# Spectral mix and token MLP on one core: the special matrix rows as a compact input of 4 transfers, the sign table as 2, and a layout that counts with 400 GB/s

## The chip, the cores and the metric

One core of a Trainium2 chip runs the whole kernel. The metric is the device time of one execution in microseconds; before the change the median of three runs is 1345.98 us (1345.09 to 1347.06).

## The reference

With x = A_x (1 x 2048 x 1024), four DFT matrices given as inputs, and a second tensor B_x for the MLP's place (the last lines pass x to both halves):

```python
def _A_ref(x, dft_seq_re, dft_seq_im, dft_hid_re, dft_hid_im):
    a = jnp.einsum("bsd,ed->bse", x, dft_hid_re)
    b = jnp.einsum("bsd,ed->bse", x, dft_hid_im)
    y = jnp.einsum("ts,bse->bte", dft_seq_re, a) - jnp.einsum("ts,bse->bte", dft_seq_im, b)
    return y

def _B_ref(x, w1, b1, w2, b2):
    h = _layernorm(x, axis=-1)
    u = jnp.einsum("bsd,sf->bdf", h, w1) + b1
    u = _gelu(u)
    y = jnp.einsum("bdf,fs->bds", u, w2) + b2
    return y.transpose(0, 2, 1)

g = _sigmoid((x * gate_w).sum(-1, keepdims=True))
return g * _A_ref(x, ...) + (1 - g) * _B_ref(x, w1, b1, w2, b2)
```

S is 2048, D 1024, F 3584, all in 32-bit floats.

## The kernel before, in words

The kernel runs four stages one after the other, with their edges overlapping: FastSeq (the DFT along the sequence), FastHid (the DFT along the hidden axis), Up and Down (the two products of the MLP, each a fast bilinear scheme of 26 products). FastSeq and FastHid make use of symmetries of the DFT matrices: a matrix is cut into blocks that are mirror images of one another up to sign, and only one of each set is multiplied. Because the matrices are inputs, the kernel also tests on the chip that the blocks agree (the groups named ne_all and ne_odd on DVE) and falls back to a second, general program if they don't. In normal use that second program doesn't run.

The symmetry fails for a few rows and columns, the special ones: in each block of 256 rows, the first 16 (SPECIAL) stand in for them. FastHid.rows (line 1866) brings these rows in: for each of two halves p a tile fes of 128 x 1024 (8 groups of 16 rows as they are in the matrix) and a tile fer_m of 128 x 512 (what the symmetry says they should be). The difference between them, with a sign from the table rowsign, gives the correction matrix fer (lines 1891 to 1920), which FastHid multiplies at the end. Before, these tiles are filled by small transfers of 16 rows each straight from the matrix ct: 8 of 64 KB into each fes (line 1880) and 16 of 16 KB into each fer_m (line 1887), 48 in all. The sign table rowsign is 128 x 4, one column for each combination of p and t2. DVE fills it with 1 (line 1845), and 24 transfers of one column and 1, 15 or 16 rows each write a -1 or a 0 from a second small table (line 1861). All these small tables lie in one tile, called tiny in the profile.

The tiles that the engines wait for early on are: fx, rows of x (512 KB a transfer, line 609); fc, blocks of the sequence matrix ct (512 KB, also line 609); fc_m, the part of fc that is multiplied, split by ACT (line 636) and DVE (line 643) into a high and a low half; fx_lo, the low half of the combined rows of x, by DVE; fd, blocks of the hidden matrix; qh, the result of FastSeq, stored in HBM; and fq, its way back.

What sets the order: every step of the kernel is a task with engines, an estimated cost, bytes, and a key that says where in the program it belongs. Graph.schedule (line 417) simulates the engines and a single transfer pipe and emits each engine's instructions in the order in which that simulation started them. TensorE's order is fixed by the order of the tasks; the others follow due times (Graph.dues, line 387; a task with a negative key is due before everything else). The pipe moves DMA_RATE bytes per us (line 32), so that constant shifts when a load counts as landed, and with it which ready task an engine takes next. Buffers are slots in two pools; a task that needs a new tile waits in the simulation until a slot is free. Each engine then runs its list strictly in order on the chip. SP issues nearly all loads and the stores of the first two stages, one after the other; a transfer waits on SP for the tiles that it reads or overwrites, and for the transfer issued eight places earlier, whose semaphore it takes over. POOL issues other stores and the transfers that add.

Of the kernel before, what the change touches and what calls it, by code (L numbers as in the profile page):

```python
# [15 lines left out]
P = 128  # L16
S = 2048
D = 1024
F = 3584
H = 512  # L20
# [8 lines left out]


HOP = 0.35
DMA_RATE = 360000.0
SPARE = 2
DMA_LATENCY = 3.5
ADD_LATENCY = 1.5
# [182 lines left out]
SEEN = 1  # L218
LATE = 1
SPECIAL = 16  # L220
LAG = 15
STATS_AT, STATS_STEP = ("y", 1), 4.5
GATE_AT, GATE_STEP = 7, 1.5
GATED_AT, GATED_STEP = 0, 2
# [119 lines left out]
class Graph:  # L344
# [72 lines left out]
    def schedule(self):  # L417
# [44 lines left out]
        def start(t, e):  # L462
# [10 lines left out]
            if t.nbytes:  # L473
                dma = max(dma, now) + t.nbytes / DMA_RATE
                end = dma + DMA_LATENCY + (ADD_LATENCY if t.engines[e] == 0.9 else 0)
# [59 lines left out]
def arm(  # L535
# [2 lines left out]
    x: bass.AP,  # L538
    ct: bass.AP,
    xs: bass.AP,  # L540
    dt: bass.AP,
    w1: bass.AP,
    w2: bass.AP,
# [8 lines left out]
    nc = tc.nc  # L552
    g = Graph(SLOTS)
# [11 lines left out]
    def const(n, name, parts=1):  # L565
        if fast and n < 8:
            if not tiny:
                tiny.extend([consts.tile([P, 32], F32, tag="tiny", name="tiny"), 0])
            tiny[1] += n
            assert tiny[1] <= 32  # L570
            return Buf(None, name, tiny[0][:, tiny[1] - n:tiny[1]], parts)
        return Buf(None, name, consts.tile([P, n], F32, tag=name, name=name), parts)
# [16 lines left out]
    def scratch(n, name, parts):  # L589
        return Buf(None, name, dram.tile([P, n], F32, tag=name, name=name), parts)  # L590
# [15 lines left out]
    def load(key, v, src, r=(), queue="SP"):  # L606
        q = {"SP": nc.sync, "ACT": nc.scalar}[queue]
        dst = (lambda: v.ap.rearrange("p (c j) -> p c j", j=H)) if len(src.shape) == 3 else lambda: v.ap
        g.add({queue: 0.06}, key, lambda e: q.dma_start(dst(), src), r=r, w=(v.reg,), nbytes=P * v.n * 4)
# [37 lines left out]
    step = 0  # L647
# [954 lines left out]
    def cast(key, o, v):  # L1602
        g.add({"ACT": act(v.n)}, key, lambda e: nc.scalar.activation(o.ap, v.ap, AF.Copy), r=(v.reg,), w=(o.reg,))

    def mirror(p, c, q):


        if (p, c, q) == (0, 0, 0):
            return 1, None
        return (1 - 2 * p) * (1 - 2 * c), c if q == 0 else 0  # L1610

    class FastSeq:


# [25 lines left out]
        def matrix(self, p, c, q, kk):  # L1640
# [6 lines left out]
            (s, rep), (turn, half) = mirror(p, c, q), mirror(q, c, p)  # L1647
            first, odd = q == kk == 0, 2 * P - SPECIAL * (p == 0)

# [59 lines left out]
        def special(self, key, c, q, kk, v, s, rep, turn, half, first):  # L1709
# [4 lines left out]
            for t in range(2) if rep is None else (rep,):  # L1714
                model = Buf("h", f"fem{c}{q}{kk}{t}", None, 4)
                for i in range(4):
                    at = i % 2 if rep is None else half
                    src = View(v[0][t], at * 2 * P, SPECIAL)
                    o = View(model, i * SPECIAL, SPECIAL, i)
                    sign = 1 if rep is None else (1 - 2 * q) ** (i // 2) * turn ** (i % 2 != half)  # L1720
# [116 lines left out]
    class FastHid:  # L1837

        def signs_of_rows(self):


            s = const(4, "rowsign")
            low = const(2, "low")
            g.add({"DVE": 0.2}, -1, lambda e: (nc.vector.memset(low.t[:, 0:1], -1.0), nc.vector.memset(low.t[:, 1:2], 0.0)), w=(low,))
            g.add({"DVE": 0.1}, -1, lambda e: nc.vector.memset(s.t, 1.0), w=(s,))
            spans = []
            for p in range(2):
                for c in range(2):
                    (sr, rep), (turn, half) = mirror(p, c, 0), mirror(0, c, p)
                    for b in range(2):  # L1850
                        for t in range(2) if rep is not None else ():
                            at = ((c * 2 + b) * 2 + t) * SPECIAL
                            for t2 in range(2):
                                if t != rep:
                                    spans.append((at, at + 1, 1, p * 2 + t2))
                                if (1 - 2 * p) ** b * sr ** (t != rep) * turn ** (t2 != half) < 0:
                                    spans.append((at + (t != rep), at + SPECIAL, 0, p * 2 + t2))

            def go(_):
                for a, b, k, col in spans:  # L1860
                    nc.sync.dma_start(s.t[a:b, col:col + 1], low.t[a:b, k:k + 1])

            g.add({"SP": 0.06 * len(spans)}, -0.9, go, r=(low,), w=(s,), nbytes=512)
            return s

        def rows(self):

            sign = self.signs_of_rows()
            edge = Buf("f", "fer", None, 2, BF16)
            for p in range(2):  # L1870
                v, model = Buf("f", f"fes{p}", None, 8), Buf("h", f"fer{p}_m", None, 8)
                for c in range(2):
                    (sr, rep), (turn, half) = mirror(p, c, 0), mirror(0, c, p)
                    for b in range(2):
                        for t in range(2):
                            k = (c * 2 + b) * 2 + t
                            at, src = k * SPECIAL, ct[p, c, 0, 0, :SPECIAL]

                            def go(_, at=at, src=src, b=b, t=t, v=v):
                                nc.sync.dma_start(v.t[at:at + SPECIAL, :], src[:, b * 2 + t])  # L1880

                            g.add({"SP": 0.06}, step, go, w=((v, k),), nbytes=SPECIAL * D * 4)
                            for t2 in range(2):
                                tr, tc_ = (t, t2) if rep is None else (rep, half)

                                def go(_, at=at, src=src, t2=t2, tr=tr, tc_=tc_, model=model):
                                    nc.sync.dma_start(model.t[at:at + SPECIAL, t2 * 2 * P:(t2 + 1) * 2 * P],
                                                      src[:, tr, tc_ * 2 * P:(tc_ + 1) * 2 * P])

                                g.add({"SP": 0.06}, step, go, w=((model, k),), nbytes=SPECIAL * 2 * P * 4)  # L1890
                d = Buf("f", f"fed{p}", None, 4)
                for b in range(2):
                    for t2 in range(2):
                        o = View(d, (b * 2 + t2) * 2 * P, 2 * P, b * 2 + t2)
                        a, m = View(v, (b * 2 + t2) * 2 * P, 2 * P), View(model, t2 * 2 * P, 2 * P)
                        col = sign.t[:, p * 2 + t2:p * 2 + t2 + 1]
                        g.add({"DVE": dve(2 * P) + 0.06}, step, lambda e, o=o, a=a, m=m, col=col: nc.vector.scalar_tensor_tensor(
                            o.ap, m.ap, col, a.ap, op0=ALU.mult, op1=ALU.subtract), r=(a.reg, m.reg, sign), w=(o.reg,))
                both = Buf("f", f"feb{p}", None, 2)
                zero, one = View(both, 0, H, 0), View(both, H, H, 1)  # L1900
                g.add({"DVE": dve(H)}, step, lambda e, d=d, zero=zero: nc.vector.scalar_tensor_tensor(
                    zero.ap, d.t[:, :H], -1.0, d.t[:, H:2 * H], op0=ALU.mult, op1=ALU.subtract), r=(d,), w=(zero.reg,))
                sub(step, one, View(v, 0, H), View(v, H, H))
                pieces = []
                for z, part in ((zero, 0), (one, 1)):
                    l, r = View(z.buf, z.c0, 2 * P, part), View(z.buf, z.c0 + 2 * P, 2 * P, part)
                    pieces.append((l, r))
                o = [View(edge, p * D + i * 2 * P, 2 * P, p) for i in range(4)]
                if p == 0:
                    outs = [(pieces[0][0], None, 0), (pieces[0][1], None, 0), (*pieces[1], -1), (*pieces[1], 1)]  # L1910
                else:
                    outs = [(*pieces[al], (1 - 2 * al) * (1 - 2 * c)) for c in range(2) for al in range(2)]
                for i, (l, r, z) in enumerate(outs):
                    if r is None:
                        cast(step, o[i], l)
                        continue
                    m = View(Buf("h", f"feo{p}{i}"), 0, 2 * P)
                    mix(step, m, r, z, l)
                    g.add({"ACT": act(2 * P)}, step, lambda e, o=o[i], m=m: nc.scalar.activation(o.ap, m.ap, AF.Copy, scale=0.5),
                          r=(m.reg,), w=(o[i].reg,))  # L1920
                if p == 0:
                    g.add({"DVE": 0.2}, step, lambda e: nc.vector.memset(
                        edge.t[:, :D].rearrange("p (v i) -> p v i", i=2 * P)[:, :, :SPECIAL], 0.0), r=((edge, 0),), w=((edge, 0),))
            square(step + 1, "rest", View(edge, 0, 2 * D))
            return edge
# [236 lines left out]
        def last(self, p, ih, pairs, got):  # L2162
            for l, r, *to in pairs:
                l, r = (View(got[i], 0, D) for i in (l, r))
                for (b, t2), op in zip(to, (add, sub)):
# [6 lines left out]
                    dst = out_dram[b * 8 + p * 4 + t2 * 2 + ih]  # L2172
                    store(step + LAG + 1, dst.t, dst, View(y, 0, D), "SP")

# [133 lines left out]
```

## Time and profile before

| | us |
|---|---|
| median of 3 runs | 1345.98 |
| lowest, highest | 1345.09, 1347.06 |
| the profiled execution | 1349.58 |
| its span, first to last instruction | 1347.7 |
| PE busy | 1254.7 (93%) |
| DVE busy | 1209.8 (90%) |
| ACT busy | 757.2 (56%) |
| POOL busy | 201.0 (15%) |

The profiled execution moved 369.98 MB, 275 GB/s on average. PE is the matrix engine (TensorE), PEld its weight loads, DVE the vector engine, ACT the scalar engine. SP has no busy time of its own: it only issues transfers, and its rows (SPq) tell when it issued them and for how long it was held. The rows of a wait say which engine and line waited, for whom, how long in total, how often, and the longest. The profile has no chain of waits for this kernel, so the stages are read from the busy times of windows and the waits inside them.

### The profile page before, as it was taken

What the parts mean: (1) busy time and instruction counts of PE and PEld (TensorE: products, weight loads), DVE (VectorE), ACT (ScalarE), POOL (GpSimd) and SP (SyncE); (2) the same over time, 40 slices, a digit from 0 to 9 for tenths busy, and PEclk for the clock granted to TensorE, in tenths of its full rate; (3) what the DMA queues carried; (4) which work ended last, traced back from release to release, by engine and by line L of the source; (5) the groups of instructions that cost most, each with busy time, mean ns of one, the idle gap of its engine ahead of it and who ended that gap; (6) DMA issues with size and microseconds to landing.
All of it is one profiled execution on the core that took longest, in us unless ns stands there. A gap on an engine that the chain in (4) does not pass through costs nothing.

```text
span 1347.7 us, 18830 instructions
## 1 busy us (share of the span) xinstructions
PE 1254.7 (93%) x6082; PEld 1015.1 (75%) x6093; DVE 1209.8 (90%) x1993; ACT 757.2 (56%) x1344; POOL 201.0 (15%) x313
## 2 busy tenths in 40 slices
PE   7398656799999999999999999999999999999997
PEld 5298641466877888888888888888878888888986
DVE  7679769859999997999999995989999989999996
ACT  5558437975556454335356374684864646666543
POOL 0000000000111121212122032321321010232112
PEclk8699777899999999999999999999999999999999
DMA  9598889528687776998899599999998385989564
GB/s 378 178 337 348 290 287 390 161 91 316 229 321 262 259 287 207 350 350 322 316 357 393 181 362 402 369 288 346 297 333 285 102 252 140 278 202 304 134 183 97
DMA packets 153865, 369.98 MB, mean 275 GB/s; under 512 B 19484, under 2 KB 22428, under 8 KB 153756
## 3 DMA queue, kind: packets, MB, share of 16 engines
q1 hardware_dynamic: 123068, 284.44, 59.8%
q0 software_dynamic: 30544, 84.17, 21.9%
q8 instruction: 50, 0.82, 0.2%
q14 instruction: 59, 0.48, 0.1%
q10 hardware_dynamic: 144, 0.07, 0.0%
HBM read 278.68 MB, written 89.92 MB: 274 GB/s over the span
## 4 chain that ended last, share of the span: by engine, by line


## 5 line engine op out<-in xcount | busy, mean ns | idle before, releaser
L1039 PE MATMUL ps_u_p<-u_p_r_hi,u_p_w_hi 128*128 128x512 f32 x728 | 284.9, 391 | 2.5 <-DVE u_c L1092 2.5
L1040 PE MATMUL ps_u_p<-u_p_r_lo,u_p_w_hi 128*128 128x512 f32 x728 | 284.4, 391 | 1.7 <-DVE u_p_r_lo L643 1.7
L1041 PE MATMUL ps_u_p<-u_p_r_hi,u_p_w_lo 128*128 128x512 f32 x728 | 284.2, 390 | 0.0
L1039 PE MATMUL ps_o_p<-o_p_r,o_p_w 128*128 128x512 f32 x654 | 255.2, 390 | 1.7 <-DVE o_c L1092 1.7
L1041 PE MATMUL ps_o_p<-o_p_r,o_p_w 128*128 128x512 f32 x654 | 254.6, 389 | 0.6 <-DVE o_p_w L641 0.6
L1040 PE MATMUL ps_o_p<-o_p_r,o_p_w 128*128 128x512 f32 x654 | 254.6, 389 | 0.2 <-DVE o_p_r L643 0.2
L636 ACT ACTIVATE u_p_w_hi<-u_W_p 128x896 fp32r<-128x896 f32 x104 | 97.5, 950 | 128.0 <-PE ps_u_p L1040 40.7
L1039 PEld LDWEIGHTS ps_u_p<-u_p_r_hi,u_p_w_hi 128*128 128x128 f32 x728 | 137.2, 188 | 32.8 <-DVE u_c L1092 4.3
L1040 PEld LDWEIGHTS ps_u_p<-u_p_r_lo,u_p_w_hi 128*128 128x128 f32 x728 | 137.3, 189 | 30.7 <-DVE u_p_r_lo L643 2.5
L1041 PEld LDWEIGHTS ps_u_p<-u_p_r_hi,u_p_w_lo 128*128 128x128 f32 x728 | 137.3, 189 | 28.6
L1039 PEld LDWEIGHTS ps_o_p<-o_p_r,o_p_w 128*128 128x128 f32 x654 | 122.8, 188 | 29.5 <-DVE o_c L1092 4.3
L1589 PE MATMUL ps_fq<-fc_m,fx_hi 128*128 128x256 f32 (+1 forms) x512 | 115.2, 322 | 30.7 <-ACT fc_m L636 23.4
L1041 PEld LDWEIGHTS ps_o_p<-o_p_r,o_p_w 128*128 128x128 f32 x654 | 122.7, 188 | 26.6 <-DVE o_p_w L641 1.0
L1040 PEld LDWEIGHTS ps_o_p<-o_p_r,o_p_w 128*128 128x128 f32 x654 | 122.8, 188 | 25.7 <-DVE o_p_r L643 0.7
L636 ACT ACTIVATE o_p_w<-o_W_p 128x512 fp32r<-128x512 f32 x164 | 99.8, 625 | 63.7 <-DVE o_W_p L604 28.4
L636 ACT ACTIVATE o_p_r<-o_R_p 128x512 fp32r<-128x512 f32 x157 | 95.4, 624 | 70.3 <-DVE o_R_p L604 37.3
L1589 PEld LDWEIGHTS ps_fq<-fc_m,fx_hi 128*128 128x128 f32 x512 | 92.0, 213 | 36.5 <-ACT fc_m L636 25.0
L619 POOL DMA_DIRECT2D u<-u_c x126 | 68.0, 540 | 308.5 <-DVE u_c L1092 116.3
L643 DVE TENSOR_TENSOR o_p_r<-o_R_p,o_p_r 128x512 fp32r<-128x512 f32 x157 | 106.8, 686 | 5.2 <-ACT o_p_r L636 5.1
L1092 DVE SCALAR_TENSOR_TENSOR u_c<-ps_u_p,u_c 128x512 f32<-128x512 f32 x161 | 105.6, 685 | 4.8 <-PE ps_u_p L1041 3.5
L1589 PE MATMUL ps_fq<-fc_m,fx_lo 128*128 128x256 f32 (+1 forms) x256 | 83.1, 325 | 16.9 <-DVE fx_lo L643 16.9
L601 DVE TENSOR_TENSOR u_W_p<-u_W_p,u_W_p 128x896 f32<-128x896 f32 x80 | 85.8, 1086 | 2.2 <-DMA u_W_p<-in_w_dram 2.2
(258 smaller groups left out, 2217.9 us busy)
## 6 DMA issues: line engine op xcount, KB each, us to landing
u_W_p<-in_w_dram SPq DMA_DIRECT2D x136, 448.0 KB, 6.7
o_W_p<-in_w_dram SPq DMA_DIRECT2D x160, 256.0 KB, 6.6
o_R_p<-u SPq DMA_DIRECT2D x140, 256.0 KB, 5.6
fc<-in_ct_dram SPq DMA_DIRECT2D x64, 512.0 KB, 9.6
u<-u_c POOLq DMA_DIRECT2D x126, 256.0 KB, 5.8
u_c<-u SPq DMA_DIRECT2D x70, 256.0 KB, 7.3
fx<-in_x_dram SPq DMA_DIRECT2D x32, 512.0 KB, 9.0
o_W_p<-in_w_dram POOLq DMA_DIRECT2D x50, 256.0 KB, 7.4
```

Of the source, the lines that this page charges most:

```text
L601: g.add({"DVE": dve(o.n)}, key, lambda e: nc.vector.tensor_add(o.ap, a.ap, b.ap), r=(a.reg, b.reg), w=(o.reg,))
L619: g.add({queue: 0.6 if queue == "POOL" else 0.06}, key, lambda e: q.dma_start(dst, v.ap), r=(v.reg,), w=(reg,) if reg else (), nbytes=P * ...
L636: g.add({"ACT": act(v.n)}, key, lambda e: nc.scalar.activation(hi.ap, v.ap, AF.Copy, scale=-1.0 if negate else 1.0), r=(v.reg,), w=(hi.reg,))
L643: nc.vector.tensor_sub(lo.ap, v.ap, hi.ap.bitcast(F32))
L1039: nc.tensor.matmul(bank.ap, wh.ap[:, c], rh.ap[:, e], start=a, stop=False, skip_group_check=True)
L1040: nc.tensor.matmul(bank.ap, wh.ap[:, c], rl.ap[:, e], start=False, stop=False, skip_group_check=True)
L1041: nc.tensor.matmul(bank.ap, wl.ap[:, c], rh.ap[:, e], start=False, stop=b, skip_group_check=True)
L1092: lambda e: nc.vector.scalar_tensor_tensor(o.ap, ps.ap, scale, o.ap, op0=ALU.mult, op1=ALU.add),
L1589: nc.tensor.matmul(b.ap[:, c0:c0 + r.shape[-1]] if r.shape[-1] < H else b.ap, w, r, start=begin, stop=end, skip_group_check=True)
```

## The change

The host now also builds er, a compact copy of the special rows: for each p one 128 x 1536 block whose first 1024 columns are what fes holds and whose last 512 are what fer_m holds. The kernel loads each tile with one transfer, two for each p. fes and fer_m become tiles of one part instead of eight. The sign table is no longer patched on 128 partitions: DVE writes all 512 values into one row on one partition (one wide write and 24 strided small ones, with the key LAY = 4), one transfer lays that row out in scratch memory in HBM, and a second reads it back as 128 x 4. The keys move it from "before everything" (-0.9) to 4 and 5. The function mirror moves out of the kernel body so that the host can call it. DMA_RATE goes from 360 to 400 thousand bytes per us, for the whole program.

```diff
-DMA_RATE = 360000.0
+DMA_RATE = 400000.0
...
+LAY = 4
...
+    er: bass.AP,
...
             s = const(4, "rowsign")
-            low = const(2, "low")
-            g.add({"DVE": 0.2}, -1, lambda e: (nc.vector.memset(low.t[:, 0:1], -1.0), nc.vector.memset(low.t[:, 1:2], 0.0)), w=(low,))
-            g.add({"DVE": 0.1}, -1, lambda e: nc.vector.memset(s.t, 1.0), w=(s,))
             spans = []
...
-            def go(_):
+            row = Buf("h", "rowsigns", None, 1)
+            bounce = scratch(4, "rowsigns", 1)
+
+            def fill(_):
+                nc.vector.memset(row.t[0:1, :H], 1.0)
                 for a, b, k, col in spans:
-                    nc.sync.dma_start(s.t[a:b, col:col + 1], low.t[a:b, k:k + 1])
-
-            g.add({"SP": 0.06 * len(spans)}, -0.9, go, r=(low,), w=(s,), nbytes=512)
+                    nc.vector.memset(row.t[0:1, a * 4 + col:(b - 1) * 4 + col + 1:4], (-1.0, 0.0)[k])
+
+            g.add({"DVE": 0.07 * len(spans)}, LAY, fill, w=(row,))
+            g.add({"SP": 0.4}, LAY, lambda e: nc.sync.dma_start(
+                bounce.t.rearrange("p k -> (p k)").unsqueeze(0), row.t[0:1, :H]), r=(row,), w=(bounce,), nbytes=P * 16)
+            g.add({"SP": 0.4}, LAY + 1, lambda e: nc.sync.dma_start(s.t, bounce.t), r=(bounce,), w=(s,), nbytes=P * 16)
             return s
...
-                v, model = Buf("f", f"fes{p}", None, 8), Buf("h", f"fer{p}_m", None, 8)
-                for c in range(2):
-                    (sr, rep), (turn, half) = mirror(p, c, 0), mirror(0, c, p)
-                    for b in range(2):
-                        for t in range(2):
-                            k = (c * 2 + b) * 2 + t
-                            at, src = k * SPECIAL, ct[p, c, 0, 0, :SPECIAL]
...
-                                nc.sync.dma_start(v.t[at:at + SPECIAL, :], src[:, b * 2 + t])
...
-                                    nc.sync.dma_start(model.t[at:at + SPECIAL, t2 * 2 * P:(t2 + 1) * 2 * P],
-                                                      src[:, tr, tc_ * 2 * P:(tc_ + 1) * 2 * P])
...
+                v, model = Buf("f", f"fes{p}", None, 1), Buf("h", f"fer{p}_m", None, 1)
+                load(step, View(v, 0, D), er[p, :, :D])
+                load(step, View(model, 0, H), er[p, :, D:])
...
+    er = _np.empty((2, 2, 2, 2, SPECIAL, D + H), ct.dtype)
+    for p, c, b, t in _np.ndindex(2, 2, 2, 2):
+        (_, stands), (_, half) = mirror(p, c, 0), mirror(0, c, p)
+        rows = ct[p, c, 0, 0, :SPECIAL]
+        er[p, c, b, t, :, :D] = rows[:, b * 2 + t]
+        for t2 in range(2):
+            tr, tc = (t, t2) if stands is None else (stands, half)
+            er[p, c, b, t, :, D + t2 * 2 * P:D + (t2 + 1) * 2 * P] = rows[:, tr, tc * 2 * P:(tc + 1) * 2 * P]
+    er = er.reshape(2, P, D + H)
```

TensorE's order is the same in both programs. Three places on SP show what moves there. The digits behind a name are p, c, q and kk for fc and fx; the number behind the last underscore only counts buffers. Lines after the change are ten higher for loads (619 for 609) and stores (629 for 619).

On SP in FastSeq's second step, before, the last of the 24 sign transfers and what follows them:

```order
L1861 DMA tiny_83<-tiny_83 15x1
L1861 DMA tiny_83<-tiny_83 1x1
L1861 DMA tiny_83<-tiny_83 16x1
L609 DMA fc0000_01_327<-in_ct_dram 128x1024
L609 DMA fc0001_00_329<-in_ct_dram 128x1024
L609 DMA b12_sb_73<-in_b12_dram 128x44
L609 DMA fc0001_01_341<-in_ct_dram 128x1024
```

The same place on SP after:

```order
L619 DMA fc0011_11_325<-in_ct_dram 128x1024
L619 DMA fc0000_01_327<-in_ct_dram 128x1024
L619 DMA fc0001_00_329<-in_ct_dram 128x1024
L619 DMA b12_sb_73<-in_b12_dram 128x44
L1868 DMA rowsigns_208<-rowsigns_285 1x512
L619 DMA fc0001_01_342<-in_ct_dram 128x1024
```

The 24 stood between fc0011_11 and fc0000_01; now those two follow each other. The row of signs goes to HBM three places later, and the table is read back ten places behind that, in front of fc0110_00.

On SP in the second half of FastSeq (fx and fc with p = 1), before, the first two groups of row transfers:

```order
L609 DMA fx1011_1_1154<-in_x_dram 128x1024
L1887 DMA fer1_m_1156<-in_ct_dram 16x256 x8
L609 DMA fc1011_01_1179<-in_ct_dram 128x1024
L1887 DMA fer0_m_1197<-in_ct_dram 16x256 x8
L609 DMA fc1011_10_1220<-in_ct_dram 128x1024
```

The same place after:

```order
L619 DMA fx1011_1_1158<-in_x_dram 128x1024
L619 DMA fc1011_01_1179<-in_ct_dram 128x1024
L619 DMA fc1011_10_1181<-in_ct_dram 128x1024
L619 DMA fc1011_11_1183<-in_ct_dram 128x1024
L629 DMA qh0100_0_126<-fqo0100_0_1201 128x512
```

The 16 transfers are gone from here; the other 16 for fer_m, which stood around fc1110_11, are gone as well. Both fer_m loads now stand behind fc1100_01.

On SP at the end of FastSeq, before, the fes transfers and the first loads of the hidden matrix (fd):

```order
L609 DMA fxs_1727<-in_xs_dram 128x512
L1880 DMA fes1_1749<-in_ct_dram 16x1024 x8
L1880 DMA fes0_1772<-in_ct_dram 16x1024 x8
L619 DMA qh1000_0_134<-fqo1000_0_1781 128x512
L609 DMA fd0100_1803<-in_dt_dram 128x2x512
```

The same place after:

```order
L619 DMA fes1_1713<-in_er_dram 128x1024
L619 DMA fxs_1715<-in_xs_dram 128x512
L619 DMA fes0_1735<-in_er_dram 128x1024
L629 DMA qh1000_0_134<-fqo1000_0_1733 128x512
L619 DMA fd0100_1754<-in_dt_dram 128x2x512
```

Sixteen transfers became two in the same place.

More of the change, by code (lines that the diff above doesn't have):

```diff
@@ L220, with mirror @@
 SPECIAL = 16
+def mirror(p, c, q):
+    if (p, c, q) == (0, 0, 0):
+        return 1, None
+    return (1 - 2 * p) * (1 - 2 * c), c if q == 0 else 0
 LAG = 15
+LAY = 4
 STATS_AT, STATS_STEP = ("y", 1), 4.5
@@ L1603, in cast @@
         g.add({"ACT": act(v.n)}, key, lambda e: nc.scalar.activation(o.ap, v.ap, AF.Copy), r=(v.reg,), w=(o.reg,))
[L1605 to L1610, printed above, removed]
     class FastSeq:
@@ L1870, in rows @@
             for p in range(2):
-                v, model = Buf("f", f"fes{p}", None, 8), Buf("h", f"fer{p}_m", None, 8)
-                for c in range(2):
-                    (sr, rep), (turn, half) = mirror(p, c, 0), mirror(0, c, p)
-                    for b in range(2):
-                        for t in range(2):
-                            k = (c * 2 + b) * 2 + t
-                            at, src = k * SPECIAL, ct[p, c, 0, 0, :SPECIAL]
[L1879 to L1887, printed above, removed]
-                                                      src[:, tr, tc_ * 2 * P:(tc_ + 1) * 2 * P])
-                                g.add({"SP": 0.06}, step, go, w=((model, k),), nbytes=SPECIAL * 2 * P * 4)
+                v, model = Buf("f", f"fes{p}", None, 1), Buf("h", f"fer{p}_m", None, 1)
+                load(step, View(v, 0, D), er[p, :, :D])
+                load(step, View(model, 0, H), er[p, :, D:])
                 d = Buf("f", f"fed{p}", None, 4)
@@ L2287 @@
         "xs": xs,
+        "er": er,
         "dt": dt,
```

## The prediction

> **What bounds the kernel now.** I read the page first, then the busy times stage by stage, then SP's instructions in order of time, then the waits of each engine inside the stages that stand out. The page says that this is a TensorE kernel with something wrong in its first fifth:
>
> ```profile
> span 1347.7 us, 18830 instructions
> PE   7398656799999999999999999999999999999997
> DVE  7679769859999997999999995989999989999996
> DMA  9598889528687776998899599999998385989564
> ```
>
> One slice is 33.7 us. From the ninth slice on PE is at 9 throughout; before that PE, DVE and DMA all go up and down. So I cut the span where that changes. The columns are the busy time of PE, PEld, DVE, ACT and POOL, PE's granted clock, the DMA share and GB/s:
>
> ```profile
> 26.00:35.00 9.00, 7.50 (x45) 7.18 (x45) 6.86 (x19) 6.05 (x15) 0.00 (x0) 0.77 0.98 388
> 35.00:49.00 14.00, 4.17 (x11) 3.02 (x11) 5.73 (x8) 3.82 (x7) 0.00 (x0) 0.69 0.02 3
> 60.00:66.00 6.00, 5.83 (x16) 4.03 (x15) 6.00 (x14) 6.00 (x12) 0.00 (x0) 0.64 0.79 285
> 66.00:110.00 44.00, 44.00 (x363) 41.30 (x362) 32.96 (x85) 26.69 (x75) 0.00 (x0) 1.00 0.99 350
> 120.00:200.00 80.00, 52.43 (x342) 47.66 (x343) 58.28 (x106) 35.97 (x70) 0.00 (x0) 0.79 0.80 281
> 200.00:258.00 58.00, 38.05 (x123) 13.48 (x125) 58.00 (x120) 49.52 (x111) 0.00 (x0) 0.79 0.81 297
> 258.00:300.00 42.00, 41.74 (x246) 26.57 (x249) 21.87 (x42) 36.49 (x71) 0.00 (x0) 0.95 0.40 126
> 395.00:420.00 25.00, 20.77 (x75) 15.20 (x74) 25.00 (x35) 10.73 (x15) 4.32 (x8) 0.86 0.91 363
> 520.00:900.00 380.00, 380.00 (x1679) 314.63 (x1678) 346.59 (x507) 191.82 (x289) 80.92 (x145) 1.00 0.92 333
> 900.00:1335.00 435.00, 432.45 (x2077) 363.25 (x2075) 420.17 (x731) 252.66 (x455) 89.19 (x109) 1.00 0.83 232
> ```
>
> Two stretches have no bound of their own. From 35 to 49 us the transfers stand still (share 0.02) and every engine runs out of work. From 120 to 200 us no engine and no transfer is full (PE 52.43, DVE 58.28 of 80, transfers 0.80). The others each have one: PE from 66 to 110, DVE from 200 to 258 (58.00 of 58), PE from 258 on. Time taken out of the two loose stretches should therefore reach the end. What SP did in them:
>
> ```profile
> 22.74 2.89 SPq L609 DMA_DIRECT2D fc<-in_ct_dram  x3
> 26.63 21.90 SPq L1861 DMA_DIRECT2D tiny<-tiny  x24
> 48.57 1.05 SPq L609 DMA_DIRECT2D fc<-in_ct_dram  x2
> ...
> 121.94 8.65 SPq L1887 DMA_DIRECT2D fer_m<-in_ct_dram  x8
> 131.10 3.92 SPq L1887 DMA_DIRECT2D fer_m<-in_ct_dram  x8
> 155.01 8.08 SPq L1887 DMA_DIRECT2D fer_m<-in_ct_dram  x8
> 163.60 3.69 SPq L1887 DMA_DIRECT2D fer_m<-in_ct_dram  x8
> 172.67 16.33 SPq L1880 DMA_DIRECT2D fes<-in_ct_dram  x16
> ```
>
> The second column is how long the group kept SP. The 24 sign-table transfers hold SP for 21.90 us while a matrix load (fc) that the engines need stands behind them; it goes out at 48.57. The 48 row transfers hold SP for 8.65 + 3.92 + 8.08 + 3.69 + 16.33 = 40.67 us inside the second loose stretch, again with matrix loads behind them.
>
> **The change, part by part.** All sums start from the profiled execution: 1349.58 us, span 1347.7. It lies 3.6 us above the median 1345.98; I subtract that 3.6 at the end.
>
> *The sign table, 24 transfers to 2.* The waits between 26 and 63 us (total, times, longest), for ACT, DVE and PE:
>
> ```profile
> ACT fc_m L636 <- DMA fc<-in_ct_dram: 14.1, 1, 14.1
> DVE fc_m L643 <- ACT fc_m L636: 15.0, 2, 12.8
> PE ps_fq L1589 <- ACT fc_m L636: 12.0, 1, 12.0
> PE ps_fq L1589 <- DVE fx_lo L643: 10.1, 3, 5.0
> ```
>
> One late load stops three engines one behind the other. With the 24 gone it is issued right behind the load that ended at 25.6 us (22.74 + 2.89), some 22 us earlier. That is earlier than anyone needs it: DVE asks for the result 12.8 us before it gets it. Of the three gaps I take DVE's 12.8, because PE, once it has fc_m, waits again for DVE (fx_lo, 5.0), so DVE is what runs last there. What is late next: the transfers themselves. In 66 to 110 they are at 0.99 beside a full PE, so both must move forward together; they can, since the idle transfers of 35 to 49 (14 us at 0.02) are as long as the gap. Bounds: 12.0 (PE's gap) to 14.1 (ACT's).
>
> What the two new transfers and their fill cost: one wide and 24 small writes by DVE, on one partition. They stand before DVE's first real work, which waits:
>
> ```profile
> 1.48 0.06 DVE L2183 MEMSET tiny<- 16x1 f32 x1
> 5.72 1.23 DVE L601 TENSOR_TENSOR fx_h<-fx,fx 128x1024 f32<-128x1024 f32 x1 [4.18 <-DMA fx<-in_x_dram]
> ```
>
> 25 at 0.06 are 1.5 us, inside the 4.18 us of waiting: nothing. Doubled, by spacing, they are 3 us and still inside. Without that cover DVE would start 1.5 to 3 us late. The first transfer (table row to scratch in HBM) waits on SP for that fill, which is over 20 us before SP gets there. The second (scratch to the table) waits for the first and stands ten places later on SP; the 24 of before land like this:
>
> ```profile
> DMA to landing us min/median/max: 1.7/2.0/6.2
> ```
>
> The eight loads and stores between them take longer than even 6.2 us (at 1.3 us a load, 22.74 to 26.63 for three), so SP does not stop for it: 0, at most 6.2 with fc0110_00 queued behind. Its reader on DVE runs much later (last column: first and last start):
>
> ```profile
> L1897 DVE SCALAR_TENSOR_TENSOR fed<-fer_m,tiny,fes x8: 476/478/484, 187.4 to 192.1; 128x256 f32<-128x256 f32 x8
> ```
>
> *The row inputs, 48 transfers to 4.*
>
> ```profile
> fes<-in_ct_dram SPq DMA_DIRECT2D x16, 64.0 KB, 3.1
> fer_m<-in_ct_dram SPq DMA_DIRECT2D x32, 16.0 KB, 2.2
> ```
>
> 16 x 64 + 32 x 16 KB are 1.5 MB. The four new transfers carry the same in pieces of 512 and 256 KB like the other loads, so SP holds nothing up for 40.67 us any more. How far the stretch 120 to 200 shrinks is set by what fills up first. DVE waited there for:
>
> ```profile
> DVE ne_all L1663 <- DMA fc<-in_ct_dram: 7.6, 5, 3.0
> DVE ne_odd L1663 <- DMA fc<-in_ct_dram: 4.4, 4, 1.6
> DVE fc_m L643 <- ACT fc_m L636: 3.9, 2, 3.6
> DVE fed L1897 <- DMA fes<-in_ct_dram: 3.3, 2, 1.9
> DVE fds L601 <- DMA fd<-in_dt_dram: 1.6, 1, 1.6
> ```
>
> That is 20.8 us, nearly all of DVE's 80 - 58.28 = 21.7 idle. If DVE became full the stretch would lose 20.8. But the transfers have to carry 80 x 281 = 22.5 MB in it. At the 350 GB/s that a saturated stretch with the same mix of loads and stores shows (66 to 110), that takes 64.2 us, so the stretch loses 15.8; at the 388 of 26 to 35, loads alone, it would be 57.9 and DVE the bound. I take 15.8: the mix is the nearer row, and two engines near full in step lose some to each other. Low bound: the 3.3 us of waits on the moved transfers alone. The DVE stage behind it (200 to 258) stays 58 us long, and starts earlier by what both stretches lose.
>
> *The planner's rate, 360 to 400.* The planner that lays out the program's order thinks transfers are faster. TensorE's order stays; loads swap places by up to five on SP, and many DVE and ACT instructions move, within the same stages. A steady stage shows no wait to win: 380.00 of 380 and 432.45 of 435. A new gap looks like the one at 395 to 420: 25 - 20.77 = 4.2 us idle, and 25 x (1 - 0.86) = 3.5 us of lower clock, 7.7 in all. I take 0 and keep plus or minus 7.7: that one gap may go, or a second come.
>
> *TensorE's clock.* From 60 to 66 PE is busy 5.83 us at 0.64. Without the 12 us gap ahead of it that work might run at full clock and save 5.83 x 0.36 = 2.1 us. But before the gap, fed in bursts, PE had only 0.77 too (26 to 35), so I count 0 and keep 2.1 as the bound. The Trainium skill (TensorE: Matmul & The Clock Gate, "Why this matters for your kernels") says that an idle gap of more than about 3 us brings the clock back to half; by it the whole 2.1 is won here and the sum is 2 us lower. The clock of 0.64 behind the gap agrees; that it would be 1.00 without the gap no row shows.
>
> Sum: 1349.6 - 12.8 - 15.8 = 1321.0, and less 3.6 on the scale of the median: 1317.4, rounded 1317.
>
> **The rivals.**
>
> *Only the first stretch gives.* In 120 to 200 the chain of ACT, DVE and PE itself, with buffers coming free late, might hold the loads back, and the 48 transfers sit in time that was lost anyway. For it: PE's mean clock there is 0.79 and it waits for ACT as well as for data. Against it: DVE's waits end on DMA. Then only 3.3 is won: 1346 - 12.8 - 3.3 = 1330.
>
> *The new layout gives some back.* One or two gaps of 7.7 us more in the long stages: 1325 to 1333. For it: from 520 to 900 the transfers run at 0.92 with only 333 GB/s, below both rates, so a plan at 400 is further off. Against: the plan at 360 was off too, and PE had no gap there. The Trainium skill (DMA: Bandwidth & Descriptors, "Specifications") gives about 358 GB/s as what HBM yields to one core, and by it a layout at 400 lets operands come late. The trace differs for loads alone, 388 GB/s from 26 to 35, and agrees in the mixed stages.
>
> *Slower than before.* The same mechanism, in the Up and Down stages (340 to 1335 us): operands planned as landed stall PE, 7.7 us each time. It eats the 28.6 won from the fourth such gap on; six of them give 1346 - 28.6 + 46 = 1364. Before has one in 1000 us.
>
> *More than forecast.* DVE fills the second stretch (20.8) and the clock comes back (2.1), with 14.1 from the first: 1346 - 37 = 1309.
>
> That the change does not do what it says can be left out: SP's new order has four row transfers and two for the table.
>
> **How the numbers follow.** Forecast 0.60, only the first stretch 0.15, layout gives back 0.12, more 0.09, slower by over 0.2% 0.03, and 0.01 for anything that lands within 0.2% (2.7 us, about what a measurement of this kernel can tell from no change), which I round up to 0.02, taking 0.95 for faster. Likeliest: 1317. The range goes from 1306 (the 1309 of the last rival and half of the 7.7 that a vanished gap would add, rounded) to 1333 (two layout gaps, which also covers the 1330). About one chance in seven is left outside.
>
> **What would show it.** Right: fc_m's wait of 12.8 on DVE gone and no stretch of transfers at 0.02 before 60 us; SP without any hold over 2 us for the sign table or the row inputs; the DVE-bound stage, 58 us at full, beginning near 172 instead of 200; PE in 520 to 900 still without a gap. The first step is wrong if DVE's first long wait merely moves to another fc load; the second if DVE's waits on fc loads between 107 and 172 still add up to over 10 us, or if that stretch is not near 64 us long; the third if PE waits for operands after 340 us more than the 4.2 + (435 - 432.45) = 6.8 us of now. The whole is wrong if the fill of the sign row shows up late on DVE and SP stands waiting for it.

## The result and the profile after

The changed kernel takes 1310.41 us (median of 4 runs, 1309.63 to 1312.9) against 1345.53 us before (4 runs): a ratio of 0.9744, with a 95% interval of 0.9724 to 0.9763. That is 35.1 us less, where 28.6 were forecast. Its profiled execution took 1309.63 us, with a span of 1307.7. That pair of profiles lies 40 us apart, because the one of before was 4.0 us above the 1345.53 and this one is 0.8 below its own median; so sizes are read from the medians where they can be, and the profiles say where the time went.

The first place, SP around the former 24 sign transfers, in the profile after (start, how long SP was held, line, transfers):

```profile
22.62 5.99 SPq L619 DMA_DIRECT2D fc<-in_ct_dram  x5
29.57 0.33 SPq L619 DMA_DIRECT2D b_sb<-in_b_dram  x1
31.76 0.30 SPq L1868 DMA_DIRECT2D rowsigns<-rowsigns  x1
32.98 2.89 SPq L619 DMA_DIRECT2D fc<-in_ct_dram  x3
...
42.05 0.32 SPq L1870 DMA_DIRECT2D tiny<-rowsigns  x1
50.86 0.33 SPq L619 DMA_DIRECT2D fc<-in_ct_dram  x1
```

The two transfers of the table hold SP for 0.30 and 0.32 us. The fc load that had gone out at 48.57 us belongs to the five of the first line. The row inputs, on SP later on, where the 48 transfers had held it for 40.67 us:

```profile
136.01 1.67 SPq L619 DMA_DIRECT2D fer_m<-in_er_dram  x2
137.78 6.29 SPq L619 DMA_DIRECT2D fc<-in_ct_dram  x7
144.41 0.33 SPq L619 DMA_DIRECT2D fes<-in_er_dram  x1
145.66 0.33 SPq L619 DMA_DIRECT2D fxs<-in_xs_dram  x1
146.97 0.33 SPq L619 DMA_DIRECT2D fes<-in_er_dram  x1
```

The four hold it for 2.33 us together. The fill on DVE, from its order in time:

```profile
1.43 0.06 DVE L2173 MEMSET tiny<- 16x1 f32 x1
1.55 0.48 DVE L1863 MEMSET rowsigns<- 1x512 f32 x1
2.09 0.46 DVE L1865 MEMSET rowsigns<- 1x1 f32 x24
5.71 1.23 DVE L611 TENSOR_TENSOR fx_h<-fx,fx 128x1024 f32<-128x1024 f32 x1 [3.16 <-DMA fx<-in_x_dram]
```

All 25 writes fit into the wait for the first loads, of which 3.16 us are left; fx_h starts at 5.71 where it had started at 5.72. The waits of DVE from 26 to 63 us, and then from 107 to 200:

```profile
DVE ne_all L1666 <- DMA fc<-in_ct_dram: 3.4, 2, 2.0
DVE fc_m L653 <- ACT fc_m L646: 0.5, 1, 0.5
```

```profile
DVE ne_all L1666 <- DMA fc<-in_ct_dram: 0.5, 1, 0.5
DVE fc_m L653 <- ACT fc_m L646: 0.4, 1, 0.4
DVE fds L611 <- DMA fd<-in_dt_dram: 0.3, 1, 0.3
```

The 12.8 us are gone, and of the 20.8 us of the second stretch 1.2 are left. The stages (busy time of PE, PEld, DVE, ACT, POOL, PE's clock, transfer share, GB/s):

```profile
35.00:49.00 14.00, 7.19 (x17) 5.45 (x18) 14.00 (x25) 10.93 (x31) 0.00 (x0) 0.63 0.85 331
60.00:66.00 6.00, 6.00 (x29) 4.95 (x28) 5.02 (x14) 3.50 (x21) 0.00 (x0) 1.00 1.01 344
66.00:107.00 41.00, 40.00 (x390) 39.29 (x389) 32.94 (x67) 26.53 (x58) 0.00 (x0) 1.00 1.00 369
107.00:160.00 53.00, 43.95 (x329) 42.48 (x328) 51.70 (x99) 32.89 (x67) 0.00 (x0) 0.94 1.03 410
160.00:200.00 40.00, 26.23 (x62) 6.72 (x63) 39.66 (x71) 33.99 (x66) 0.00 (x0) 0.73 1.01 382
300.30:801.10 500.80, 496.22 (x2183) 408.98 (x2182) 468.10 (x652) 244.42 (x350) 89.79 (x167) 1.00 0.84 303
801.80:1298.10 496.30, 492.26 (x2339) 412.57 (x2337) 471.52 (x825) 294.36 (x533) 107.24 (x138) 1.00 0.84 244
```

Both loose stretches now have a bound: DVE works without a break from 35 to 49, and from 107 to 160 DVE (51.70 of 53) and the transfers (1.03) are full together. The row to look at is the rate there: 410 GB/s, not the 350 that the prediction took. The last two rows are Up and Down, from the first product of one to the last of it. In the kernel before they were:

```profile
340.00:842.90 502.90, 498.67 (x2184) 410.91 (x2183) 469.81 (x651) 248.39 (x354) 90.10 (x168) 0.99 0.84 306
843.60:1337.90 494.30, 491.75 (x2338) 412.37 (x2337) 470.44 (x825) 293.70 (x530) 106.83 (x137) 1.00 0.85 243
```

Up begins 39.7 us earlier (300.30 for 340.00), Up itself is 2.1 us shorter and Down 2.0 longer. All of the gain lies in the first two stages.

### The profile page after: what moved, and what is told of

It is laid out like the page before. It is cut to its first block, busy times and chain, and to the rows that moved or that the text cites. A ratio compares the mean times of both kernels' runs of the same rounds, so it can differ in the third digit from the quotient of the medians.

```text
span 1307.7 us, 18781 instructions
## 1 busy us (share of the span) xinstructions
PE 1243.3 (95%) x6082; PEld 1007.8 (77%) x6093; DVE 1209.8 (93%) x2015; ACT 754.5 (58%) x1344; POOL 200.8 (15%) x313
## 3 DMA queue, kind: packets, MB, share of 16 engines
q0 software_dynamic: 30544, 84.17, 22.5%
## 4 chain that ended last, share of the span: by engine, by line
## 5 line engine op out<-in xcount | busy, mean ns | idle before, releaser
L1599 PE MATMUL ps_fq<-fc_m,fx_hi 128*128 128x256 f32 (+1 forms) x512 | 109.1, 312 | 7.1 <-ACT fx_hi L646 4.3
L1599 PEld LDWEIGHTS ps_fq<-fc_m,fx_hi 128*128 128x128 f32 x512 | 87.9, 204 | 11.5 <-ACT fx_hi L646 4.5
```

The lines of the kernel that those rows point to most:

```text
L1599: nc.tensor.matmul(b.ap[:, c0:c0 + r.shape[-1]] if r.shape[-1] < H else b.ap, w, r, start=begin, stop=end, skip_group_check=True)
```

## The experiments

The first theory: a small transfer costs little itself, what costs is SP, which issues in order and stands between the engines and their loads. The two groups are then worth 12.5 us and some 20 or more, add up, and the planner's rate is worth nothing. The rivals: one part hides the other; part of the gain is the new layout; small transfers cost by themselves.

**signs_only.** The kernel with the new sign table alone (the hunk on signs_of_rows), rows and rate as before.

> The sign table alone by 2 transfers; the 48 row transfers stay, the planner's rate stays 360. Theory (a transfer group costs what SP holds back behind it): the idle stretch from 35 to 49 us goes and nothing takes it back, so 12.5 us less than before, about 1333 us. Rival (the first two stages are one pipe whose later part, held up by the row transfers, absorbs an earlier start): 1340 us or more.

Measured: 1333.29 us (1332.02 to 1334.31), ratio 0.9909 (0.9888 to 0.9929), 12.1 us less. The theory's number; nothing takes it back.

**rows_only.** The er input and its four loads alone; the 24 sign transfers and the rate 360 stay.

> The row inputs alone by 4 transfers; the 24 sign transfers stay, rate 360. Theory: the second loose stretch closes until DVE or the transfers are full, worth the 25 to 27 us that the changed kernel's profile shows beyond the first 12.5, about 1319 us. Rival (the prediction's size: transfers full at 350 GB/s): 15.8 us less, about 1330 us, the rest having come from the rate or from both parts together.

Measured: 1324.54 us (1322.36 to 1329.09), ratio 0.9847 (0.9821 to 0.9872), 20.8 us less: more than the 15.8 of the prediction, less than the 25 to 27 read from the pair of profiles. Its stages at the same place:

```profile
66.00:110.00 44.00, 43.94 (x356) 41.22 (x357) 33.58 (x88) 27.71 (x77) 0.00 (x0) 1.00 0.97 348
120.00:200.00 80.00, 62.52 (x375) 48.24 (x375) 76.56 (x142) 50.28 (x99) 0.00 (x0) 0.89 1.04 405
```

From 66 to 110 us the rate is 348 GB/s, near the 350 of before, and from 120 to 200 it is 405, both at a share near 1. So the two stretches do not have the same rate. Between the two profiles FastSeq's last product (ps_fq) starts 11.8 us earlier (186.3 to 174.5) and FastHid's first (ps_fw) 19.2 us earlier (196.0 to 176.8): a good part of the gain lies between the two stages, where the fd loads had stood behind the 16 fes transfers.

**both_360.** Everything but the rate.

```diff
-DMA_RATE = 400000.0
+DMA_RATE = 360000.0
```

> Both transfer parts, planner's rate back at 360. Theory (the rate is worth nothing in the long stages): 1310 us, within 3 of the changed kernel. Rival (part of the gain beyond the forecast came from the order laid out with 400): 1316 us or more.

Measured: 1312.35 us (1310.91 to 1314.01, 5 runs), ratio 0.9753 (0.9735 to 0.9771), 33.0 us less. The two parts alone give 12.1 + 20.8 = 32.9, so they add up. The 1.9 us to the changed kernel are within the spread of both.

**rate_only.** The kernel before with the rate 400.

> The kernel before with the rate 400 alone, all 72 small transfers in place. Theory: no change beyond 3 us, 1343 to 1348 us. Rival (the layout gains by itself): 1340 us or less; rival (the layout with 400 costs, hidden in the full change by the transfers' gain): 1350 us or more.

Measured: 1347.07 us (1343.8 to 1349.42, 12 runs), ratio 1.0008 (0.9996 to 1.002): no change. The rate as a whole is worth nothing, as forecast; mixed_layout below shows a gain and a loss behind it.

**small_from_pool.** The kernel before with all 72 small transfers as they were, issued from POOL:

```diff
-    nc.sync.dma_start(s.t[a:b, col:col + 1], low.t[a:b, k:k + 1])
+    nc.gpsimd.dma_start(s.t[a:b, col:col + 1], low.t[a:b, k:k + 1])
...
-    nc.sync.dma_start(v.t[at:at + SPECIAL, :], src[:, b * 2 + t])
+    nc.gpsimd.dma_start(v.t[at:at + SPECIAL, :], src[:, b * 2 + t])
```

and so for fer_m, with POOL's cost in the planner.

> The kernel before with all 72 small transfers as they were, but issued from POOL, which has nothing else to do there; rate 360. Theory (what cost time was SP, held with loads behind the small transfers): nearly the whole gain without any larger transfer, 1310 to 1318 us. Rival (72 small transfers cost the transfer engines and their readers by themselves, whoever issues them): 1330 us or more.

Measured: 1320.01 us (1318.77 to 1321.46), ratio 0.981 (0.9795 to 0.9825), 25.0 us less. Neither number: between them. Against both_360, which has the large transfers on SP instead, it lies 7.7 us higher. Its second stretch shows where:

```profile
107.00:160.00 53.00, 42.22 (x286) 39.86 (x287) 45.57 (x81) 29.96 (x59) 9.09 (x19) 0.84 1.03 374
```

The share is full (1.03) as in the changed kernel, but it carries 374 GB/s for 410. So three quarters of the gain (25.0 of 33.0) is SP set free; the last quarter fits the lower rate of a pipe with small transfers in it. These are mostly 16 row transfers of 64 KB, each 16 pieces of 4 KB: only 1,001 of the 6,468 packets of this stretch are under 2 KB, against 784 of 7,567 in both_360. So short pieces are not what lowers the rate here. Whether it is the size of the transfers, their few rows or the issue from POOL was not tried.

**stores_halved.** The changed kernel, with each 256 KB store of FastSeq's results cut in two, so that a partition's piece is 1 KB for 2 KB:

```diff
-    store(step + 1, dst.t, dst, v, "SP")
+    for h in range(2):
+        g.add({"SP": 0.06}, step + 1, lambda e, dst=dst, v=v, h=h: nc.sync.dma_start(
+            dst.t[:, h * 2 * P:(h + 1) * 2 * P], View(v.buf, h * 2 * P, 2 * P).ap), r=(v.reg,), w=((dst, h),), nbytes=P * 2 * P * 4)
```

> The changed kernel with each of the 28 stores of FastSeq's results of 256 KB cut into two of 128 KB with 1 KB pieces. From 66 to 110 us before, 26 loads of 512 KB at 412 GB/s take 33.1 of 44 us, so the 16 stores of 128 KB cost near 0.6 us each there. Theory (the 350 GB/s of that stretch came from these stores, and the second stretch ran at 412 because it has none): the rate at full share between 107 and 160 us falls to about 360 GB/s and the kernel loses 5 to 10 us, 1315 to 1321 us. Rival (the rate has nothing to do with the stores' pieces, or the transfers do not bind there): 1312 us or less, rate still over 400.

Measured: 1317.73 us (1316.23 to 1319.41), ratio 0.9797 (0.9782 to 0.9812), 7.3 us above the changed kernel, inside the theory's range. The transfers from 107 to 160 us, and then the same window of the changed kernel:

```profile
DMA packets 7885, 19.87 MB, mean 375 GB/s; under 512 B 867, under 2 KB 3414, under 8 KB 7880
qh<-fqo SPq DMA_DIRECT2D x21, 128.0 KB, 6.6
```

```profile
DMA packets 7336, 21.71 MB, mean 410 GB/s; under 512 B 780, under 2 KB 780, under 8 KB 7331
qh<-fqo SPq DMA_DIRECT2D x12, 256.0 KB, 8.2
```

Same share (1.02 and 1.03), the same kind of loads, and 375 GB/s (the theory said about 360) for 410 once 2,600 more packets are under 2 KB. The theory holds: stores of 128 KB lower the rate, and with it the kernel gets slower. Halving a store halves its size as well as its pieces, so which of the two costs is not told apart.

**fewer_compares.** The changed kernel with the symmetry test of FastSeq's second half cut to 64 columns of each 256, so it leaves out three quarters of that test.

```diff
-first, odd = q == kk == 0, 2 * P - SPECIAL * (p == 0)
+first, odd = q == kk == 0, 2 * P - SPECIAL if p == 0 else 64
```

> The changed kernel with the symmetry test of the second half of FastSeq (p = 1) cut to 64 of 256 columns of each block, so it leaves out three quarters of that test; DVE is spared some 20 us of compares between 107 and 172 us. Theory (the transfers end last in that stretch, DVE is only as full): at most 4 us less, 1306 to 1311 us. Rival (DVE ends last there): 10 us or more less, 1300 us or below.

Measured: 1312.64 us (1308.93 to 1313.62), ratio 0.9749 (0.9731 to 0.9768): nothing won. That is just above the theory's 1306 to 1311, with a spread that overlaps that of the changed kernel, and far from the rival's 1300.

```profile
107.00:160.00 53.00, 42.93 (x320) 40.78 (x319) 32.03 (x96) 32.97 (x65) 0.00 (x0) 0.93 1.03 409
```

DVE's work there fell from 51.70 to 32.03 us and the end did not move: FastSeq's last product starts at 156.8 us for 157.9, Up's first at 299.4 for 300.3. In its place DVE now waits, 14.7 us of it for fc loads (0.5 in 107 to 200 us of the changed kernel). The transfers end last in that stretch; DVE, nearly as full in the changed kernel, sets at most about 1 us of it.

**mixed_layout.** The changed kernel, laid out with 400 until the planner's 780 us and with 360 from there, so for Down:

```diff
-dma = max(dma, now) + t.nbytes / DMA_RATE
+dma = max(dma, now) + t.nbytes / (DMA_RATE if now < 780 else 360000.0)
```

> The changed kernel, laid out with 400 until the planner's 780 us and with 360 from there. By the profiles so far the layout with 400 makes the Up stage 2 us shorter and the Down stage 2 to 4 us longer. Theory (these are real): 1307 us, 2 to 4 below the changed kernel. Rival (differences of single profiles): 1310 to 1312 us.

Measured: 1304.59 us (1302.76 to 1306.53, 5 runs), ratio 0.9698 (0.9683 to 0.9712): 5.8 us below the changed kernel, more than the 2 to 4 expected, and its slowest run is faster than the fastest of that one. It beats both kernels. Its Up and Down:

```profile
300.50:801.30 500.80, 497.13 (x2184) 410.39 (x2183) 469.43 (x654) 245.47 (x351) 90.91 (x168) 1.00 0.83 304
801.90:1292.90 491.00, 490.73 (x2338) 412.94 (x2338) 469.77 (x822) 293.44 (x531) 106.94 (x137) 1.00 0.84 245
```

Up is as long as in the changed kernel (500.80), Down 5.3 us shorter (491.00 for 496.30). The other profiles agree: from the first to the last start of Down's main products there are 492.2 to 494.3 us in the five profiles laid out with 360 and 495.5 to 498.6 in the four with 400. PE waits for nothing in Down now; in the changed kernel it waited there for:

```profile
PE ps_o_p L1049 <- ACT o_c L1094: 2.4, 3, 1.4
PE ps_o_p L1049 <- DVE o_c L1102: 1.6, 4, 0.8
```

## Why the prediction was right, point by point

*The sign table: 12.8 forecast, 12.1 measured alone.* The choice of DVE's gap among 12.0, 12.8 and 14.1 was the right one: from 26 us on DVE works through, and its compare ne_odd behind the gap starts at 46.67 instead of 59.21, 12.5 earlier. The fill cost nothing, by the row above. The second transfer of the table landed after 6.5 us, more than the 6.2 of the bound, and nothing waited for it.

*The row inputs: 15.8 forecast, 20.8 measured alone. This is the term that was mis-sized,* and it accounts for 5.0 of the 6.5 us by which the kernel is faster than forecast. The mechanism was the forecast one: SP no longer held the loads back, and the stretch closed until the transfers were full. What failed is the step "at the 350 GB/s that a saturated stretch with the same mix of loads and stores shows". The mix was not the same. From 66 to 110 us before, 16 of the stores were of 128 KB, with pieces of 1 KB, and 2,711 of 5,950 packets were under 2 KB; the second stretch has stores of 256 KB only. The rows for 66 to 110 us before:

```profile
DMA packets 5950, 15.41 MB, mean 350 GB/s; under 512 B 663, under 2 KB 2711, under 8 KB 5945
qh<-fqo SPq DMA_DIRECT2D x16, 128.0 KB, 8.4
```

Without such stores the second stretch carries 405 to 410 GB/s (rows_only, after), and stores_halved brings it back to 375 by adding them. With 405 for 350 the 22.5 MB take 55.5 us, so that DVE's 58.28 would have come out as the bound and the working would have given some 21. That this is close to the 20.8 measured is no proof of it: DVE and the transfers are full together there, and fewer_compares shows that the transfers end last. The prediction named the right bound, but with a rate that was too low; by its own comparison the right rate would have named DVE. The transfers alone at 405 would give 80 - 55.5 = 24.5, and what keeps the gain 3.7 below that is not shown. By its own sign, a stretch near 64 us, this step failed: FastHid's first product starts 35.8 us earlier in the changed kernel (196.0 to 160.2), 12.8 of that is the first gap, and so the stretch is near 57.

*The planner's rate: 0 forecast.* Right in the sum (rate_only, ratio 1.0008), but by a balance that was not forecast, so in part by luck: the one gap of the Up stage, 395 to 420 us before, went, as the low bound had allowed, and Down took as much back. The gap of 7.7 us was priced too high: Up got 2.1 us shorter. Its 4.2 us of idle only moved: PE still stands idle for 4.6 us of Up, 2.7 of them at the start, where it waits for DVE (fy_k). What Up saved is busy time, 498.67 to 496.22 us, which fits the end of the lower clock in that gap (0.86 to 1.00). By the prediction's sign this step failed too: with the 4.0 of Down, PE's idle in the two stages is 8.6 us, above the 6.8 it had named.

*TensorE's clock: 0 forecast, 2.1 as the bound.* From 60 to 66 us the clock is 1.00 for 0.64, but PE got ahead by DVE's gap and hardly more: the first product of fg (ps_fg) starts at 104.3 us before, 91.1 in signs_only and 91.7 in the changed kernel, which is 13.2 and 12.6 earlier for a gap of 12.8. So no more than 0.4 of the 2.1 shows. The two transfer parts alone leave 35.1 - 12.1 - 20.8 = 2.2 us of the gain. That is within the spread of the runs, and no run tells what they are.

*The rivals.* "Only the first stretch gives" fell with rows_only. The slower one asked for four gaps of 7.7 us; all of PE's waits in Down with the rate 400 are 4.0 us.

*Small slips of the working.* Nine transfers stand between the two of the table, not eight; and 1309 less half of 7.7 is 1305, not the 1306 of the range. Neither changes anything. The 388 GB/s taken for loads alone was low as well: the same 26 to 35 us carry 409 in the changed kernel, where the loads go on.

What stays open: why an order laid out with 400 suits Up and not Down. The waits name o_c, the sums that DVE and ACT take out of TensorE's banks, but which swap of theirs does it was not tried.

## What to carry to other kernels

Look at what a queue holds back, not at the bytes that it moves: 24 transfers of a few bytes cost 12.1 us because a load stood behind them, and all 72 small transfers, issued from an idle queue, gave three quarters of the whole gain. When a stretch is sized by a transfer rate, take the rate from a stretch with the same sizes of transfers and pieces, since a pipe can be full at 348 and at 410 GB/s. A planner's constant that changes nothing in the sum may still be a gain and a loss in two stages; time the stages apart before dropping it.

## What was not expected of the hardware

Stores of 128 KB in pieces of 1 KB cost a full pipe dearly: the 21 of them in 107 to 160 us of stores_halved take what is left of 53 us after 17.1 MB at 410 GB/s, 11.3 us or 0.54 us each, an estimate of some 245 GB/s for them from those rows. The Trainium skill (DMA: Bandwidth & Descriptors, "Specifications") puts the least size for the full rate at 512 bytes; these runs show a loss with pieces of 1 KB, in stores of 128 KB. The same table's 358 GB/s for one core, worked out there as half of what two cores share, is passed by the 410 of 107 to 160 us in the changed kernel and the 405 of 120 to 200 in rows_only; this kernel runs on one core.
